# Which engine issues the two turned copies of the second softmax's weights: ScalarE instead of SyncE

## The chip, the cores and the metric

One Trainium2 chip, one of its cores. The metric is device time in microseconds (us), the median over runs of the whole program. The kernel is a single launch; all its intermediate arrays stay on the chip or in its own HBM buffers.

## The reference

Three computations follow one another. The inputs have 8 batches, 8 heads, 576 rows and head dimension 64; 32 "packed" queries stand in `p`.

```python
def sm_attn(qq, kk, vv):
    s = scale * np.matmul(qq, kk.transpose(0, 1, 3, 2))
    s = s - np.max(s, axis=-1, keepdims=True)
    a = np.exp(s)
    a = a / (np.sum(a, axis=-1, keepdims=True) + 1e-09)
    return np.matmul(a, vv)
p_packed = sm_attn(p, k, v)              # first softmax: 32 packed rows per head
out = sm_attn(q, p_packed, p_packed)     # second softmax: 576 rows over 32 columns
# x = out as [4608, 512]
rms = np.sqrt(np.mean(x * x, axis=-1, keepdims=True) + 1e-06)
xn = x / rms * rms_g
g = xn @ w_gate; val = xn @ w_val        # d_ff = 1536
y = (g / (1 + np.exp(-g)) * val) @ w_out
final = ((y @ w1) * (y @ w2) @ w3) @ w_out2
```

The attention's output is never built: the kernel multiplies the packed values into the gate and value weights (tiles `wbh`, `wbl`) and multiplies these by the second softmax's transposed, normalised weights `a2T` (split into `ah`, `al`). The RMS of a row is found from the softmax weights as well, with a small Gram matrix `G` of the packed values: the sum of squares of a row is a2T * (G a2T), summed over 32 columns and 8 heads.

## The kernel before, in words

The order of the work on every engine is written out by hand (`manual_schedule`, line 76): each engine runs its instructions strictly in the order in which the Python program issues them, and that holds for DMA issues too. Every DMA of the kernel is issued by SyncE (SP). A DMA that has to wait for data therefore holds back every DMA that comes after it in the program.

The stretch that matters is the first third, some 20 to 460 us, in which attention and the gate/value layer run together for batch after batch:

- `dense_units` (lines 418 to 454) is the main loop. One batch has 48 steps, here called units and numbered on through the batches. A unit is six matmuls of 128x288 (line 432) into one of four PSUM banks (`bank`, line 55). An even unit ends in a tanh on ScalarE (ACT, line 438) and a multiply on VectorE (DVE, line 439, "stt" below); an odd one, from batch 1 on, in a copy on ACT (line 447, tile `vl`) and a multiply on GpSimd (POOL, line 448, tile `ht`), in batch 0 in a multiply on DVE (line 444). After the fourth unit of each group of eight, `wb_unit` (lines 383 to 397) makes the next group's weights: matmuls on line 391, then `split` (lines 58 to 60), that is `wbh` on ACT (line 59) and `wbl` on DVE (line 60). Results `ht` go to HBM by `store_later` and `stores` (lines 402 to 409).
- `unpack(b)` (lines 284 to 378) is the second softmax of batch b. It is a generator with 18 steps, and `planned` (lines 490 to 497) takes its steps between the units of the batch before, at the numbers in `PLAN` and `UNPACK` (lines 533 to 542). Steps 0 to 6 compute the scaled exponentials. Step 7 transposes one half of them on DVE (line 327, e = 1) and issues the two copies that the change is about (lines 330 and 331). Step 8 transposes the other half (e = 0). Step 9 multiplies by `G` on TensorE (PE, line 343), sixteen matmuls by `a2T` and sixteen by `turned`, and takes the products on DVE (line 348).
- `turned` is `a2T[:, 1]` moved up by 32 partitions, the last 32 rows last, so that the matmuls of both halves can sit in different quarters of the array. It is made for batches 1 to 7, so there are 14 copies: seven of 96 rows and seven of 32, each row 2304 bytes. `turned` has one buffer.
- `pack(b)` (lines 202 to 279) is the first softmax; its last step copies `G` on ACT (line 277), its first has reductions on DVE (line 218) and exponentials on ACT (line 221).
- Weights come as 64-bit words and are converted: load (line 106), two ACT instructions (lines 113 and 114), two on DVE (lines 120 and 121), one on POOL (line 123).

In the program's order step 7 of `unpack` stands right behind the tanh of one unit: unit 20 for batch 1, unit 76 for batch 2, and units 112, 160, 208, 256 and 304 for batches 3 to 7. Step 8 follows at once for batches 3 to 7, at unit 21 for batch 1 and at unit 79 for batch 2. Step 9 stands behind unit 24 for batch 1, unit 81 for batch 2, and units 119, 167, 215, 263 and 311 after that. For batch 2, step 0 of `pack(3)` stands at unit 78, between steps 7 and 8.

After about 460 us the output projection and the bilinear layers follow; nothing in them is touched.

Of the kernel before, what the change touches and what calls it, by code (L numbers as in the profile page):

```python
# [32 lines left out]
def packed_attention_swiglu_bilinear(ctx: ExitStack, tc, qT, kT, v, v_end, pT, rms_g, w_gv, w_out,  # L33
                                     w1, w2, w3T, w_out2, out):
    nc = tc.nc
# [248 lines left out]
    def unpack(b):  # L284
# [21 lines left out]
        for a, t in enumerate(ts):  # L306
            nc.vector.transpose(out=a2.rearrange("p e t n -> p e (t n)")[:, :, HALF * a:HALF * a + HALF],
                                in_=t[:, :, :HALF])
# [15 lines left out]
        a2T = att.tile([128, 2, S], F32, tag="a2T", name="a2T")  # L324
        order = (0, 1) if b == 0 else (1, 0)
        for e in order:
            nc.vector.transpose(out=a2T[:, e], in_=a2[:, e].rearrange("p t n -> p (t n)"))
            if b and e:
                turned = att.tile([128, S], F32, tag="turned", name="turned")
                nc.sync.dma_start(out=turned[:96], in_=a2T[32:, 1])  # L330
                nc.sync.dma_start(out=turned[96:], in_=a2T[:32, 1])
            yield

        assert ("made", b) in over
# [184 lines left out]
    def spin():  # L519
        while True:  # L520
            t = bank()
            for _ in range(4):
                nc.tensor.matmul(t[:, :128], lhsT=ident, rhs=ident, start=True, stop=True)
            yield

    gens = dict(x=spin(), p=pack(0), u=unpack(0), c=gvw, d=gvd, w=wb_first(), l=later(), P=pack(1), U=unpack(1),
                Q=pack(2), V=unpack(2), R=pack(3), o=ow)
    for x in ("pxxpxdxcxppdpcdpccdxcuduudcxuldupuxcuuw"
              "xxxxxdxlcuxxxxxxdcuuduuuPxlPPluPuxuuPldP"):
# [16 lines left out]
    for b in range(2, B - 1):  # L546
        if b + 2 < B:
            steps.append(([48 * b + n for n in PACK], pack(b + 2)))
        steps.append(([48 * b + n for n in UNPACK], unpack(b + 1)))
        steps.append(([48 * b + n for n in WOUT], ow))  # L550
# [560 lines left out]
```

## Time and profile before

| what | value |
|---|---|
| median of 3 runs | 1348.25 us (1348.1 to 1349.21) |
| the profiled execution: its own time | 1346.48 us |
| its span, first to last instruction | 1344.6 us |
| mean granted TensorE clock | 0.996 |
| busy: PE / DVE / ACT / POOL | 98% / 65% / 43% / 41% |
| PE's tenths in the 40 slices | 7 in the first, 8 in the third and the last, 9 or more else |
| granted clock's tenths in the 40 slices | 8 in the third slice (67 to 101 us), 9 or more else |

The page gives busy time by engine, the span in 40 slices, the DMA queues, the chain of waits that ended last, and the costliest groups of instructions. Of the trace, timelines of single engines, the waits of one tile, the chain of waits in a window and busy time by stretch are used below. In a timeline the bracket behind a row is the engine's idle time before it and what ended it. SPq is SyncE's queue of DMA issues.

### The profile page before, as it was taken

The numbers are of one execution on the slowest core, as the hardware profiler recorded it, in microseconds if no ns is written. First come the engines' busy times: TensorE is split into PE (matmuls) and PEld (weight loads), VectorE is DVE, ScalarE is ACT, GpSimd is POOL, SyncE is SP. The second block draws the span as 40 slices with busy tenths as digits, with TensorE's granted clock in tenths as the row PEclk, the third lists the DMA queues.
The fourth block names the chain that finished last, engine by engine and source line by source line (L and its number), as shares of the span: only waits on it lengthen the run. The fifth ranks groups of instructions, "written<-read, shape, count | busy, mean of one in ns | idle before, by whom it ended". The sixth has DMA issues, their size and how long they took to land.

```text
span 1344.6 us, 23644 instructions
## 1 busy us (share of the span) xinstructions
PE 1322.6 (98%) x9010; PEld 1124.2 (84%) x9010; DVE 875.4 (65%) x1286; ACT 577.7 (43%) x1117; POOL 557.4 (41%) x467
## 2 busy tenths in 40 slices
PE   7989999999999999999999999999999999999998
PEld 6768888888888888888888888888888888899998
DVE  5796677777776557727475664578459657657645
ACT  5645566667666655525243442124015103305113
POOL 3341446656556542203221313445345335435442
PEclk9989999999999999999999999999999999999999
DMA  9855467647342576724399885656755856787875
GB/s 342 305 187 199 152 219 255 218 160 265 125 160 104 166 243 225 241 81 156 107 379 388 316 278 210 223 209 225 263 203 200 287 187 219 249 299 262 282 272 185
DMA packets 88706, 304.04 MB, mean 226 GB/s; under 512 B 9872, under 2 KB 14992, under 8 KB 74384
## 3 DMA queue, kind: packets, MB, share of 16 engines
q1 hardware_dynamic: 88592, 302.52, 63.9%
q8 instruction: 71, 1.16, 0.4%
q14 instruction: 43, 0.35, 0.1%
HBM read 223.87 MB, written 76.55 MB: 223 GB/s over the span
## 4 chain that ended last, share of the span: by engine, by line
PE 88%; DVE 7%; DMA 2%; issue 2%; ACT 1%; POOL 0%; SPq 0%; DVEq 0%; ACTq 0%; POOLq 0%
PE gv L432 21%; PE gv L946 13%; PE at L946 13%; PE at L636 12%; PE gv L636 7%; PE gv L1040 5%; PE at L1040 5%; PE at L391 3%; PE gv L736 3%; DVE sl L60 1%; PE at L214 1%; DVE wbl L60 1%; PE at L343 1%; PE at L245 1%; PE at L359 1%
## 5 line engine op out<-in xcount | busy, mean ns | idle before, releaser
L448 POOL TENSOR_TENSOR ht<-th,vl 128x288 f32<-128x288 f32 x168 | 138.9, 836 | 121.2 <-ACT vl L447 68.9
L432 PE MATMUL gv<-ah,wbh 128*128 128x288 f32 x768 | 174.5, 308 | 4.6 <-DVE th L439 3.9
L432 PEld LDWEIGHTS gv<-ah,wbh 128*128 128x128 f32 x768 | 121.2, 188 | 55.9 <-issue 22.5
L432 PE MATMUL gv<-al,wbh 128*128 128x288 f32 x768 | 164.7, 295 | 0.0
L432 PE MATMUL gv<-ah,wbl 128*128 128x288 f32 x768 | 164.1, 295 | 0.0
L60 DVE TENSOR_TENSOR hl<-hr,hh 128x512 fp32r<-128x512 f32 x108 | 101.3, 943 | 75.1 <-ACT hh L59 72.9
L972 POOL TENSOR_TENSOR s<-uc 128x512 f32<-128x512 f32 (+1 forms) x40 | 49.0, 1224 | 231.6 <-DVE uc L928 231.6
L946 PE MATMUL gv<-xh,w 128*128 128x512 f32 (+1 forms) x560 | 137.8, 367 | 0.0
L946 PE MATMUL at<-xh,w 128*128 128x512 f32 (+1 forms) x560 | 137.7, 367 | 0.0
L123 POOL TENSOR_TENSOR c_o<-c_o,c_y 128x512 int32<-128x512 int32 x52 | 71.0, 1366 | 146.2 <-DVE c_o L121 124.8
L439 DVE SCALAR_TENSOR_TENSOR th<-th,gv 128x288 f32<-128x288 f32 x192 | 84.9, 445 | 61.6 <-ACT th L438 52.4
L432 PEld LDWEIGHTS gv<-al,wbh 128*128 128x128 f32 x768 | 123.4, 188 | 0.0
L432 PEld LDWEIGHTS gv<-ah,wbl 128*128 128x128 f32 x768 | 123.3, 188 | 0.0
L59 ACT ACTIVATE hh<-hr 128x512 fp32r<-128x512 f32 x108 | 67.6, 629 | 115.2 <-PE at L636 60.1
L946 PEld LDWEIGHTS gv<-xh,w 128*128 128x128 f32 x560 | 102.5, 188 | 13.4
L946 PEld LDWEIGHTS at<-xh,w 128*128 128x128 f32 x560 | 102.5, 188 | 13.3
L636 PE MATMUL at<-hl,wo_h 128*128 128x512 f32 x288 | 112.1, 389 | 0.0
L636 PE MATMUL at<-hh,wo_l 128*128 128x512 f32 x288 | 112.1, 389 | 0.0
L636 PE MATMUL at<-hh,wo_h 128*128 128x512 f32 x288 | 112.0, 389 | 0.0
L438 ACT ACTIVATE th<-gv 128x288 f32<-128x288 f32 x192 | 78.7, 410 | 53.2 <-PE gv L432 51.8
L447 ACT ACTIVATE vl<-gv 128x288 f32<-128x288 f32 x168 | 69.2, 412 | 50.1 <-PE gv L432 35.1
L60 POOL TENSOR_TENSOR xl<-yi,xh 128x1024 fp32r<-128x1024 f32 (+1 forms) x20 | 57.3, 2872 | 74.0 <-ACT xh L59 49.9
(164 smaller groups left out, 2836.1 us busy)
## 6 DMA issues: line engine op xcount, KB each, us to landing
w<-ws_d SPq DMA_DIRECT2D x40, 1024.0 KB, 5.0
w<-w_d SPq DMA_DIRECT2D x35, 1024.0 KB, 4.8
w<-ws_d SPq DMA_DIRECT2D x40, 768.0 KB, 4.6
hT_d<-ht SPq DMA_DIRECT2D x96, 288.0 KB, 3.5
hr<-hT_d SPq DMA_DIRECT2D x108, 256.0 KB, 4.9
w<-in_w_gv_dram SPq DMA_DIRECT2D x24, 512.0 KB, 6.1
w<-in_w_out_dram SPq DMA_DIRECT2D x20, 512.0 KB, 5.0
q<-in_qT_dram SPq DMA_DIRECT2D x8, 1152.0 KB, 7.6
```

What stands on the lines that cost most here:

```text
L59: nc.scalar.activation(out=hi, in_=src, func=AF.Copy)
L60: eng_lo.tensor_tensor(out=lo, in0=src, in1=hi.bitcast(F32), op=ALU.subtract)
L123: nc.gpsimd.tensor_tensor(out=d, in0=d, in1=shape(y), op=ALU.add)
L432: nc.tensor.matmul(t[:, :HALF], lhsT=w[:, e, 256 * i + 128 * f:256 * i + 128 * f + 128], rhs=x[:, e, HALF * hf:HALF * hf + HALF], start=(n ...
L438: nc.scalar.activation(out=th, in_=t[:, :HALF], func=AF.Tanh, scale=0.5)
L439: nc.vector.scalar_tensor_tensor(out=th, in0=th, scalar=1.0, in1=t[:, :HALF], op0=ALU.add, op1=ALU.mult)
L447: nc.scalar.activation(out=vl, in_=t[:, :HALF], func=AF.Copy, scale=0.5)
L448: nc.gpsimd.tensor_tensor(out=ht[:, hf], in0=th, in1=vl, op=ALU.mult)
L636: nc.tensor.matmul(acc[m], lhsT=w[:, kk, 128 * m:128 * m + 128], rhs=x, start=(kk == 0 and a == 0), stop=(kk == NF - 1 and a == 2))
L946: nc.tensor.matmul(t, lhsT=wi[:, r, pos, a], rhs=x[:, j, r, :w], start=(start and at == 0), stop=(at == 5), skip_group_check=True)
L972: nc.gpsimd.tensor_tensor(out=s2, in0=u2, in1=c22, op=ALU.mult)
L1040: nc.tensor.matmul(t, lhsT=wi[:, s, k, 128 * m:128 * m + 128], rhs=x, start=(j in (0, 5, 4, 3) and k == 0 and n == 0), stop=(k == 3 and n ...
```

## The change

The two copies into `turned` are issued by ScalarE's queue. Source, destination and place in the program stay as they are; the copies now stand in ACT's order, behind the tanh of the unit named above and ahead of the next ACT instruction, and no longer in SyncE's.

```diff
             nc.vector.transpose(out=a2T[:, e], in_=a2[:, e].rearrange("p t n -> p (t n)"))
             if b and e:
                 turned = att.tile([128, S], F32, tag="turned", name="turned")
-                nc.sync.dma_start(out=turned[:96], in_=a2T[32:, 1])
-                nc.sync.dma_start(out=turned[96:], in_=a2T[:32, 1])
+                nc.scalar.dma_start(out=turned[:96], in_=a2T[32:, 1])
+                nc.scalar.dma_start(out=turned[96:], in_=a2T[:32, 1])
             yield
```

## Rows read from the trace of the kernel before

**Rows 1.** The page, busy us (share of the span) and instructions by engine.
```profile
PE 1322.6 (98%) x9010; PEld 1124.2 (84%) x9010; DVE 875.4 (65%) x1286; ACT 577.7 (43%) x1117; POOL 557.4 (41%) x467
```
**Rows 2.** The page, the chain that ended last, shares of the span by engine.
```profile
PE 88%; DVE 7%; DMA 2%; issue 2%; ACT 1%; POOL 0%; SPq 0%; DVEq 0%; ACTq 0%; POOLq 0%
```
**Rows 3.** Tile `turned`: count, ns min/median/max, first and last start; landing in us.
```profile
L330 SPq DMA_DIRECT2D turned<-a2T x7: 527/532/583, 81.7 to 409.1; - x7
L331 SPq DMA_DIRECT2D turned<-a2T x7: 587/587/594, 82.3 to 409.7; - x7
...
DMA to landing us min/median/max: 2.5/2.7/3.0
```
**Rows 4.** Waits of SyncE's queue, 60 to 440 us: total, times, longest.
```profile
SPq L330 <- DVE a2T L327: 40.8, 5, 8.2
```
**Rows 5.** Timeline of DVE, batch 2's copies: start, length, instruction, idle before.
```profile
148.05 0.77 DVE L327 STREAM_TRANSPOSE a2T<-a 128x576 f32<-128x576 f32 x1
148.74 0.42 DVE L439 SCALAR_TENSOR_TENSOR th<-th,gv 128x288 f32<-128x288 f32 x1
...
150.87 0.77 DVE L327 STREAM_TRANSPOSE a2T<-a 128x576 f32<-128x576 f32 x1
152.58 0.46 DVE L439 SCALAR_TENSOR_TENSOR th<-th,gv 128x288 f32<-128x288 f32 x1 [0.94 <-ACT th L438]
```
**Rows 6.** Timeline of ACT around batch 2's copies.
```profile
147.97 0.41 ACT L438 ACTIVATE th<-gv 128x288 f32<-128x288 f32 x1 [0.32 <-PE gv L432]
...
151.78 0.40 ACT L447 ACTIVATE vl<-gv 128x288 f32<-128x288 f32 x1
152.07 0.41 ACT L438 ACTIVATE th<-gv 128x288 f32<-128x288 f32 x1
```
**Rows 7.** Chain of waits, 140 to 160 us: start, length, what.
```profile
151.78 1.38 PE at L343 x31
```
**Rows 8.** Timeline of SyncE's queue around batch 3's copies.
```profile
195.07 0.59 SPq L331 DMA_DIRECT2D turned<-a2T  x1
```
**Rows 9.** Timeline of ACT around batch 3's copies.
```profile
194.40 0.41 ACT L438 ACTIVATE th<-gv 128x288 f32<-128x288 f32 x1 [0.33 <-PE gv L432]
...
196.28 1.03 ACT L59 ACTIVATE wbh<-at 128x1024 fp32r<-128x1024 f32 x1
197.20 0.41 ACT L438 ACTIVATE th<-gv 128x288 f32<-128x288 f32 x1
```
**Rows 10.** Timeline of DVE around batch 3's copies.
```profile
197.34 1.23 DVE L60 TENSOR_TENSOR wbl<-at,wbh 128x1024 fp32r<-128x1024 f32 x1 [0.78 <-ACT wbh L59]
198.49 0.44 DVE L439 SCALAR_TENSOR_TENSOR th<-th,gv 128x288 f32<-128x288 f32 x1
```
**Rows 11.** Timeline of PE after batch 3's copies.
```profile
199.49 0.45 PE L343 MATMUL at<-turned,G 32*32 32x288 f32 x4
...
200.60 0.53 PE L432 MATMUL gv<-ah,wbh 128*128 128x288 f32 x2
```
**Rows 12.** Timeline of ACT around batch 1's copies.
```profile
76.86 0.42 ACT L438 ACTIVATE th<-gv 128x288 f32<-128x288 f32 x1
...
78.55 0.25 ACT L277 ACTIVATE G<-at 128x64 f32<-128x64 f32 x1
82.87 0.41 ACT L438 ACTIVATE th<-gv 128x288 f32<-128x288 f32 x1 [4.07 <-PE gv L432]
```
**Rows 13.** Chain of waits, 60 to 110 us.
```profile
83.89 2.24 PE at L343 x24
...
90.80 6.02 DMA hT_d<-ht
```
**Rows 14.** Timeline of DVE around the landing of that store.
```profile
96.95 0.46 DVE L444 SCALAR_TENSOR_TENSOR ht<-th,gv 128x288 f32<-128x288 f32 x1 [1.89 <-DMA hT_d<-ht]
```
**Rows 15.** Stretches: PE, PEld, DVE, ACT, POOL busy; granted clock, DMA share, GB/s.
```profile
78.00:82.00 4.00, 2.03 (x10) 1.80 (x11) 3.90 (x8) 0.80 (x3) 2.32 (x2) 0.88 0.00 0
81.00:83.90 2.90, 1.81 (x8) 1.50 (x9) 2.87 (x6) 0.97 (x2) 1.12 (x1) 0.51 0.29 90
```

## The prediction, made before the run

> **What bounds the kernel now.** I read the page's busy times first: PE is busy 98% of the span, every other engine 65% or less [rows 1]. The chain that ended last agrees, 88% of it is PE, and SyncE's queue has 0% [rows 2]. So a moved DMA issue saves nothing by itself, and what the change is worth is decided where PE waits. Next I took the waits of the tile `turned`. An issue takes SyncE 0.53 and 0.59 us, and the copies land 2.5 to 3.0 us after it [rows 3]. Then the waits of SyncE's queue: at five of the seven places it stands at line 330 for up to 8.2 us until DVE has made the transpose [rows 4]. SyncE has nothing else to do; ACT has. Last I read the timelines of ACT, DVE and PE at the seven places, because after the change ACT must stand still from the tanh ahead of the copies until the transpose is there, and for the two issues besides.
>
> **What is removed.** Seven times two issues leave SyncE, 7 x 1.12 = 7.8 us of its time, and its five long waits, 40.8 us [rows 3, 4]. All of it lies off the chain. What stood behind them (stores of `ht`, loads of weight words) can be issued sooner.
>
> **What is added to ACT, per place.** The wait for the transpose, then the two issues. In the trace the second issue starts 0.6 us after the first (82.3 after 81.7) and takes 0.59, so SyncE's pair takes 1.2 us [rows 3]. No ACT issue is in the trace. Bounds: 0, if ACT handed the issues on and went ahead at once, and 2.4, twice SyncE's pair, if an engine with work of its own in flight issues more slowly. I take 1.2, the same instruction's own row.
>
> **Batch 2, the term that decides.** Step 7 stands behind the tanh of unit 76, and the `vl` copy of unit 77, the tanh of unit 78 and everything after them now wait. The transpose ends at 148.05 + 0.77 = 148.82 [rows 5]; with 1.2 ACT is free at 150.02. The `vl` copy goes first, and the tanh follows 0.29 later, the spacing of the same two instructions at 151.78 and 152.07 [rows 6]: the tanh of unit 78 starts at 150.31 and not at 147.97. DVE's multiply (stt) starts 0.51 after a tanh that it waits for (152.07 to 152.58) [rows 5, 6], so at 150.82 and not at 148.74: 2.08 later. Behind it in DVE's order are the reductions of `pack(3)` and the second transpose at 150.87, with no idle time before it [rows 5], so the second transpose ends 2.08 later, and it is the one that PE's line 343 waits for at 151.78, where the chain of waits goes from DVE to PE [rows 7]. PE has no bracket of idle time there now, it will have one of 2.1 us, and after it PE is busy without slack. **+2.1**; with a pair of 0 it is +0.9, with 2.4 it is +3.3. The turned copies are not late then: their issues end at about 150.0 in both kernels, and 3.0 us after the second one's start they have landed [rows 3], ahead of 153.9.
>
> **Batches 3 to 7: five places with the same order, covered barely.** Batch 3's rows stand for all. SyncE's second issue ends at 195.07 + 0.59 = 195.66 [rows 8], and ACT's would too. Then it has one `vl` copy (0.29), and from the tanh at 194.40 to `wbh` at 196.28 there are 1.88 us without a gap [rows 9], so `wbh` starts at 195.66 + 2.17 = 197.83, 1.55 late, and so do the next tanh and DVE's `wbl`. `wbl` would start at 198.89 and the stt behind it at 198.49 + 1.55 = 200.04, ending at 200.48 [rows 10]. PE's next group starts at 200.60 [rows 11]; it needs `wbl` and the bank that this stt empties. Slack 0.1 us: **0 each**, and whatever the pair costs above 1.3 us comes out of PE five times over. The copies end their issue when they ended before and land about 197.6; they are first read at 199.49 [rows 3, 8, 11], 1.9 us of cover. I put **+0.2** for the five, since a slack of 0.1 is within what I can read.
>
> **Batch 1.** ACT runs far ahead of DVE here. The tanh of unit 20 starts at 76.86 and the copy of `G` ends at 78.80; ACT then idles 4.07 us [rows 12]. After the change ACT stands from 77.3 until the issues end at 82.3 + 0.59 = 82.9 [rows 3], and then still has this work, 1.94 us less the tanh's own 0.3: 1.6. `G` is ready at 84.5, line 343 starts 0.7 later than 83.89 [rows 13]. But 7 us on, the chain of waits leaves the engines: a store of `hT_d` issued at 90.80 takes 6.02 us to land [rows 13] and holds DVE's next `ht`, idle for 1.89 us [rows 14]. The DMA engines had stood at 0.00 from 78 to 82 [rows 15], while SyncE's queue waited at line 330. Loads that stood behind it start earlier now, so the store meets a shorter queue. Late by 0.7, some 0.9 with what DVE adds, and early by 0 to 1.9, DVE's idle time there: between -1.0 and +0.9. **0.**
>
> **Sum.** 2.1 + 0.2 + 0 = 2.3 us on the profiled execution's 1346.48: 1348.8. The median of the runs shown lies 1.77 above that execution, so I predict 1348.25 + 2.3 = **1350.5 us**, slower by 0.17%. What a measurement of this kernel can tell from no change is about 0.2%, 2.7 us; the forecast is a loss just inside it.
>
> A rule for the transfers: SyncE's copies land 2.5 to 3.0 us after issue [rows 3]. The Trainium skill ("DMA: Bandwidth & Descriptors", section "Issuing engines are not separate DMA queues") says that DMAs issued from different engines run on the same 16 DMA engines and interleave, so that issuing from several only saves the issue time. By that rule alone the copies land as before and the sum would be 0, rival C below. The rule counts what the issuing engine no longer does; SyncE's 8.2 us of standing [rows 4] show that an engine also pays with its wait, and by those rows the sum is 2.3.
>
> **Rivals.**
> - *A, every place stops PE.* If the pair on ACT takes 2.0, two thirds of the way to its upper bound, batch 2 costs 2.9, and each of batches 3 to 7 0.8 - 0.1 = 0.7: 2.9 + 3.5 + 0.3 for batch 1 = 6.7, so 1354.9. For it: the slack of 0.1 that I found at five places. Against: it needs ACT slower at an issue than SyncE. It decides from a pair of 1.3 us on.
> - *B, the clock falls.* PE's new 2.1 us of idle time at batch 2 are followed by small matmuls. At batch 1 the granted clock stood at 0.51, the 1.2 GHz level, from 81.0 on, after a stretch in which PE was busy 2.03 of 4.00 us [rows 15]. Then line 343's 1.38 us [rows 7] and about as much behind it take double: 2.3 + 1.4 to 2.8, about 1352.6. Against: PE is fully busy ahead of batch 2.
> - *C, ACT's standing is hidden and the time stays.* If issues on ACT let the next instruction through, batch 2 costs 0.9, which batch 1's earlier loads can pay: 1348.3. For it: ACT is busy 43% only [rows 1]. Against: DVE's row without a gap behind the tanh at batch 2.
> - *D, faster.* SyncE's queue, no longer held, brings the store of 90.80 in 1.9 us earlier and takes as much from each of some further stores that POOL waits for; with batch 2 at 0.9 that is at least 2.8 us off: 1345.4. It decides where the store lands before about 95. Against: PE is the chain nearly throughout [rows 2], so there is little left for POOL to give.
>
> **Chances.** Forecast 0.50 (its own range 1349.0 to 1351.8: a pair between 0.3 and 1.4, and batch 1's spread), A 0.18, B 0.10, C 0.16, D 0.06. The forecast's upper third lies past 2.7 us: slower 0.16 + 0.18 + 0.10 = 0.44. Within 0.2%: 0.34 + 0.16 = 0.50. Faster: 0.06. The range that leaves out D and the far part of A is 1347.6 to 1354.5.
>
> **What would show it.** ACT rows at line 330 and 331 with a wait up to the transpose and a pair of about 1.2 us; at batch 2 a PE gap of about 2 us before line 343 (151 to 154 us) with the second transpose some 2.1 us later; no PE gap before line 432 after line 343 at batches 3 to 7; SyncE's queue without a wait at line 330 and the store of about 91 us landing in under 6 us. I am wrong if the gap at batch 2 is under 1 us, if gaps of over 0.3 stand at batches 3 to 7, or if the granted clock falls anywhere past 100 us.

## The result, and the profile after

| what | before | changed |
|---|---|---|
| median, us | 1348.17 (1347.98 to 1349.21) | 1360.54 (1359.15 to 1361.12, 4 runs) |
| ratio, 95% interval | | 1.0093 [1.0081, 1.0105] |
| span of the profiled execution, us | 1344.6 | 1358.8 |

The change costs 12.4 us. The prediction said 2.3, with a range up to 1354.5: right in sign, wrong by a factor of five.

The page after: busy times, the granted clock in 40 slices, the new DMA queue (packets, MB, share), the chain by engine.

```profile
PE 1333.2 (98%) x9010; PEld 1130.3 (83%) x9010; DVE 873.7 (64%) x1286; ACT 575.3 (42%) x1117; POOL 558.9 (41%) x467
...
PEclk9889899999999999999999999999999999999999
...
q10 hardware_dynamic: 1120, 2.07, 0.5%
...
PE 84%; DVE 5%; DMA 2%; issue 1%; ACT 1%; ACTq 0%; SPq 0%; DVEq 0%
```

Beside [rows 1, 2] this looks like the same kernel: ACT is no busier and its queue has 0% of the chain. PE is "busy" 10.6 us longer with as many instructions: most of the loss hides there, as matmuls that take longer, and not as idle time.

To find the places, I cut both executions at the end of each batch's first transpose into `a2T` (start plus length in DVE's timelines, as 148.05 + 0.77 in [rows 5]):

| stretch, us | before | changed | more |
|---|---|---|---|
| start to batch 1's transpose (no copy yet) | 81.66 | 83.77 | +2.1 |
| batch 1 to 2 | 67.16 | 67.61 | +0.5 |
| batch 2 to 3 | 45.64 | 53.38 | +7.7 |
| batches 3 to 7, four stretches | 54.32, 54.31, 54.32, 51.60 | 55.13, 55.26, 54.96, 52.26 | +0.8, +0.9, +0.6, +0.7 |
| batch 7's to the end | 935.6 | 936.4 | +0.8 |

The first line isn't the change's: it ends before the first copy, and over all kernels profiled here, SyncE's or ACT's copies, that point lies between 81.4 and 84.4. (Near 42 us the granted clock is at half for 3.41 us in the profile before, for 6.83 in the changed one, and not at all in two of the others.) The rest is 0.5 for batch 1, 7.7 for batch 2 and 3.9 for batches 3 to 7: 12.1.

**Batch 2.** ACT's timeline of the changed kernel, to be read against [rows 6]:

```profile
148.98 0.40 ACT L438 ACTIVATE th<-gv 128x288 f32<-128x288 f32 x1
151.42 0.55 ACTq L330 DMA_DIRECT2D turned<-a2T  x1
152.01 0.61 ACTq L331 DMA_DIRECT2D turned<-a2T  x1
152.73 0.41 ACT L447 ACTIVATE vl<-gv 128x288 f32<-128x288 f32 x1 [3.35 <-PE gv L432]
153.03 0.41 ACT L438 ACTIVATE th<-gv 128x288 f32<-128x288 f32 x1
```

DVE's, against [rows 5]:

```profile
150.61 0.77 DVE L327 STREAM_TRANSPOSE a2T<-a 128x576 f32<-128x576 f32 x1
153.47 0.45 DVE L439 SCALAR_TENSOR_TENSOR th<-th,gv 128x288 f32<-128x288 f32 x1 [2.08 <-ACT th L438]
...
155.55 0.77 DVE L327 STREAM_TRANSPOSE a2T<-a 128x576 f32<-128x576 f32 x1
```

ACT stands from 149.38 until the transpose is there (150.61 + 0.77) and then for its pair, 151.42 to 152.62. The tanh, DVE's multiply and the second transpose come late one after the other. That much is the predicted chain. PE's timeline shows what it led to. First the row ahead of line 343 in the profile before, which ends 0.15 us ahead of that line's start at 151.78 [rows 7]; then the changed kernel:

```profile
151.21 0.42 PE L432 MATMUL gv<-ah,wbl 128*128 128x288 f32 x2
```

```profile
156.47 0.45 PE L343 MATMUL at<-a2T,G 32*32 32x288 f32 x4 [2.22 <-DVE a2T L327]
...
158.29 0.68 PE L343 MATMUL at<-turned,G 32*32 32x288 f32 x1 [1.00 <-DMA turned<-a2T]
158.30 0.71 PE L343 MATMUL at<-a2T,G 32*32 32x288 f32 x4
...
160.35 0.85 PE L432 MATMUL gv<-ah,wbh 128*128 128x288 f32 x2
```

Three losses stand in these rows: the gap of 2.22 that was predicted; a second gap of 1.00 for a copy that isn't there; and, from 157.76 on, matmuls of 0.85 that take 0.53 elsewhere [rows 11]. The last is the clock, in the stretch's granted value (columns as in [rows 15]):

```profile
157.76:168.00 10.24, 8.91 (x56) 5.67 (x56) 3.24 (x7) 3.23 (x6) 2.23 (x3) 0.50 0.15 55
```

For 10.24 us TensorE runs at 0.50, its 1.2 GHz level. For the second gap SyncE's queue and the landings point to a cause; the run that holds SyncE, below, tests it. SyncE's k load before, then the changed kernel's timeline:

```profile
151.23 0.40 SPq L87 DMA_DIRECT2D k<-in_kT_dram  x1
```

```profile
151.76 0.33 SPq L87 DMA_DIRECT2D k<-in_kT_dram  x1
152.18 0.57 SPq L106 DMA_DIRECT2D w<-in_w_out_dram  x1
```

The DMAs issued from 151 to 159 us: KB each, and us from issue to landing:

```profile
k<-in_kT_dram SPq DMA_DIRECT2D x1, 1152.0 KB, 6.3
...
w<-in_w_out_dram SPq DMA_DIRECT2D x1, 512.0 KB, 7.0
turned<-a2T ACTq DMA_DIRECT2D x1, 216.0 KB, 3.3
turned<-a2T ACTq DMA_DIRECT2D x1, 72.0 KB, 6.2
```

SyncE, no longer held by the copies, issues its k load 0.25 us ahead of ACT's second copy; before, the load went out 2.4 us behind the transpose's end and behind both copies. ACT's second copy, the smallest of the four transfers, takes 6.2 us to land and not 2.5.

**Batches 3 to 7.** Line 343's first and last rows at batch 3 before ([rows 11] have a row between):

```profile
199.47 0.45 PE L343 MATMUL at<-a2T,G 32*32 32x288 f32 x4
...
200.25 0.42 PE L343 MATMUL at<-turned,G 32*32 32x288 f32 x4
```

The changed kernel, ACT's first issue and PE's timeline:

```profile
204.79 0.53 ACTq L330 DMA_DIRECT2D turned<-a2T  x1
```

```profile
209.78 0.69 PE L343 MATMUL at<-a2T,G 32*32 32x288 f32 x8
210.64 0.44 PE L343 MATMUL at<-turned,G 32*32 32x288 f32 x4 [0.17 <-DVE wbl L60]
210.67 0.44 PE L343 MATMUL at<-a2T,G 32*32 32x288 f32 x4
...
211.15 0.66 PE L343 MATMUL at<-turned,G 32*32 32x288 f32 x8
```

DVE's row that releases it:

```profile
209.36 1.23 DVE L60 TENSOR_TENSOR wbl<-at,wbh 128x1024 fp32r<-128x1024 f32 x1 [0.62 <-ACT wbh L59]
```

Line 343 starts 4.99 us after the first issue (204.79), as before. But before, the matmuls of `turned` start 0.02 behind those of `a2T` and run beside them; here they start 0.86 later, at `wbl`'s end (210.59). The products of `a2T` go to one slot of `at` and those of `turned` to the other; the second slot still holds the projected weights that `wbl` reads. From its first start to its last end line 343 takes 2.03 us here and 1.84 to 2.15 at the five places, against 1.20 before. Hardly a bracket shows it, since PE is busy with the first half. The waits of the tile `turned` do, on the weight loads' side; before the change this view has no such line:

```profile
  DVE wbl L60: 3.7, 7
```

3.7 us in seven waits, all of them at these five places, which lose 3.9 in all.

### The profile page after: what moved, and what is told of

It is laid out like the page before. It is cut to its first block, busy times and chain, and to the rows that moved or that the text cites. A ratio compares the mean times of both kernels' runs of the same rounds, so it can differ in the third digit from the quotient of the medians.

```text
span 1358.8 us, 23626 instructions
## 1 busy us (share of the span) xinstructions
PE 1333.2 (98%) x9010; PEld 1130.3 (83%) x9010; DVE 873.7 (64%) x1286; ACT 575.3 (42%) x1117; POOL 558.9 (41%) x467
## 3 DMA queue, kind: packets, MB, share of 16 engines
q10 hardware_dynamic: 1120, 2.07, 0.5%
## 4 chain that ended last, share of the span: by engine, by line
PE 84%; DVE 5%; DMA 2%; issue 1%; ACT 1%; ACTq 0%; SPq 0%; DVEq 0%
PE gv L432 19%; PE gv L946 13%; PE at L946 13%; PE at L636 12%; PE gv L636 7%; PE at L1040 5%; PE gv L1040 5%; PE gv L736 3%; PE at L391 3%; DVE sl L60 1%; PE at L343 1%; DVE wbl L60 1%; DMA hr<-hT_d 1%; PE at L245 1%; DVE hl L60 1%
```

## The experiments

Theory T, from here on: three mechanisms, each at its own place. At batch 2, ACT's standing makes a first gap, the freed SyncE a second, and the clock falls behind them; at batches 3 to 7 it is the slot; at batch 1 nothing lasts.

**The change in parts.** In place of the two `nc.sync` lines stands the following, with the condition `b == 2`, `b > 2` or `b == 1`:

```diff
-                nc.sync.dma_start(out=turned[:96], in_=a2T[32:, 1])
-                nc.sync.dma_start(out=turned[96:], in_=a2T[:32, 1])
+                eng = nc.scalar if b == 2 else nc.sync
+                eng.dma_start(out=turned[:96], in_=a2T[32:, 1])
+                eng.dma_start(out=turned[96:], in_=a2T[:32, 1])
```

> Copies of batch 2 alone on ACT. Theory T (the loss is made at the places, batch 2 the largest): PE waits 2.2 us for DVE's second transpose and 1.0 for the 32-row copy ahead of line 343, and the granted clock stands at 0.5 for some 10 us behind it, which is 7.7 of the 14.2 us of the profiles: +6 to +8.5 us. Rival Q (a second hardware queue in use costs about 2 us wherever it is used, and the rest is spread evenly over the seven places, 1.7 each): +3.5 to +4.

> Copies of batches 3 to 7 alone on ACT. T: at each of the five places line 343 stands 0.65 to 0.95 us in the middle, for the PSUM slot that wbl on DVE has not read yet: +3.3 to +4.7 us, no fall of the clock. Q: +2 and five times 1.7: about +10.

> Copies of batch 1 alone on ACT. T: line 343 starts 0.8 later, the later store wait takes most of it back, 0 to +1 us; up to +2.5 if the clock at 0.5 near 85 us lasts longer, as it did with all copies moved. Q: +3.5 to +4.

A fourth run moves none of the copies, only one small load at the start, so that the second queue exists:

```diff
-    nc.sync.dma_start(out=gT, in_=rms_g)
+    nc.scalar.dma_start(out=gT, in_=rms_g)
```

> All copies on SyncE as before; only the load of the four columns of rms_g at the start is issued by ACT, so that a second hardware queue is in use and nothing waits for it. T: 0, within 1 us. Q: +2 us, the amount by which the profile of the changed kernel was late before its first copy.

| ACT issues | median, us | ratio to before (1346.55) |
|---|---|---|
| batch 2's copies | 1353.86 | 1.0054 [1.0036, 1.0072] |
| batches 3 to 7's | 1351.56 | 1.0032 [1.0021, 1.0043] |
| batch 1's | 1349.13 | 1.0009 [0.9999, 1.0020] |
| one other load | 1347.84 | 1.0002 [0.9993, 1.0012] |

(The ratio is estimated from all runs; it is not the quotient of the two medians.) By the ratios the first three add up to 7.3 + 4.3 + 1.2 = 12.8 us; the whole change has 12.4. So no sign shows that the parts help or hurt each other, and the second queue by itself costs nothing that can be told. Rival Q's 3.5 to 4, 10, 3.5 to 4 and 2 us stand outside all four intervals. PE's gaps with batch 2 alone:

```profile
153.16 0.70 PE L344 MATMUL at<-a2T,G 32*32 32x288 f32 x4 [2.22 <-DVE a2T L327]
...
155.01 0.68 PE L344 MATMUL at<-turned,G 32*32 32x288 f32 x1 [0.53 <-DMA turned<-a2T]
```

The stretch at the lower clock there, columns as above:

```profile
152.95:159.78 6.83, 6.09 (x43) 3.40 (x43) 1.63 (x4) 1.62 (x6) 1.58 (x2) 0.50 0.46 167
```

The stretch from batch 2 to 3 is 6.0 longer; the gaps, less the 0.15 that before has there, are 2.6 of it. Of the other 3.4 the clock has about 3.0, half of the 6.09 us in which PE was busy at 0.50; that is an estimate, and 0.4 stays open.

**The gap filled.** Batch 2's copies on ACT, and 16 products of the identity, into a bank that is not read, ahead of line 343:

```diff
+        if b == 2:
+            t = bank()
+            for _ in range(16):
+                nc.tensor.matmul(t[:, :128], lhsT=ident, rhs=ident, start=True, stop=True)
```

> Batch 2's copies on ACT as in the run with batch 2 alone (1353.9 us, +7.3), and 16 small matmuls of the identity on PE in the 2.2 us in which it waits ahead of line 343; their result is not used. Theory T (of batch 2's loss some 3 us are standing, the rest is the granted clock that falls to 0.5 behind the standing): the clock stays at 1 past 150 us, and +2.5 to +4 is left. Rival S (the clock falls because of the small 32x32 matmuls and whatever late data does, not because PE stood still): no change, +6 to +8.

1351.85 us, 1.0029 [1.0018, 1.0040]. PE:

```profile
154.13 3.73 PE L340 MATMUL gv<-ident 128*128 128x128 f32 x32
...
158.83 0.42 PE L348 MATMUL at<-turned,G 32*32 32x288 f32 x1 [0.33 <-DMA turned<-a2T]
```

The filler is 1.5 us longer than the gap, and yet the stretch is 1.8 shorter than without it (49.90 against 51.67): the granted clock is 1.00 from 101 to 1350 us. The clock's part is real: 1.8 + 1.5 = 3.3 us by the two traces, 4.9 by the times (7.3 less 3.9, and the 1.5).

**The wait without the issues.** SyncE's copies stay; behind them ACT reads one column of the same transpose, so that it stands as long but issues nothing:

```diff
+                seen = att.tile([128, 1], F32, tag="seen", name="seen")
+                nc.scalar.activation(out=seen, in_=a2T[:, 1, :1], func=AF.Copy)
```

> All copies on SyncE as before; at the same place ACT gets one tiny activation that reads a column of the transposed half, so ACT waits for the transpose and issues nothing. T (ACT's standing delays what is behind it): at batch 2 line 343 waits 2.2 less the 1.2 to 1.5 of the issues, 0.7 to 1.0; at batches 3 to 7 wbl is 0.3 to 0.6 late and the 0.9 us of slack of its PSUM slot hold; the clock stays: +0.5 to +2. Rival W (the waits alone are the loss, the issues are free): +10 to +12.

1346.93 us, 1.0001 [0.9992, 1.0011], before 1347.74. PE's row at batch 2:

```profile
151.78 0.45 PE L345 MATMUL at<-a2T,G 32*32 32x288 f32 x4 [1.05 <-DVE a2T L327]
```

The gap is 1.05 and not 0.15: +0.9, the figure that the prediction had for a pair of 0. No place of batches 3 to 7 loses anything (54.31 to 54.32 again). The wait alone costs at most 1.5 us, so rival W falls; what breaks the slack at batches 3 to 7 comes with the issues.

**The issues without the wait.** All copies on ACT, each behind work that ACT does after the transpose anyway: one step later in the lists of due units (22 at batch 1, 78 at batch 2, 20 at batches 3 to 7, where line 343's step goes from 23 to 26):

```diff
-                nc.sync.dma_start(out=turned[:96], in_=a2T[32:, 1])
-                nc.sync.dma_start(out=turned[96:], in_=a2T[:32, 1])
             yield
+            if b and (e == 0 if b != 2 else e == 1):
+                nc.scalar.dma_start(out=turned[:96], in_=a2T[32:, 1])
+                nc.scalar.dma_start(out=turned[96:], in_=a2T[:32, 1])
+                yield
...
-            ("U", [13, 15, 15, 16, 17, 18, 19, 20, 21, 24, 25, 28, 32, 34, 42, 42, 43, 45]),
+            ("U", [13, 15, 15, 16, 17, 18, 19, 20, 21, 22, 24, 25, 28, 32, 34, 42, 42, 43, 45]),
...
-            ("V", [63, 64, 67, 68, 72, 72, 73, 76, 79, 81, 82, 82, 84, 84, 87, 89, 91, 94]),
+            ("V", [63, 64, 67, 68, 72, 72, 73, 76, 78, 79, 81, 82, 82, 84, 84, 87, 89, 91, 94]),
...
-    UNPACK = [-1, -1, 0, 2, 7, 8, 12, 16, 16, 23, 24, 25, 30, 30, 35, 36, 38, 43]
+    UNPACK = [-1, -1, 0, 2, 7, 8, 12, 16, 16, 20, 26, 26, 26, 30, 30, 35, 36, 38, 43]
```

> All 14 copies on ACT, but at places where ACT need not wait for the transpose: batch 1 two units later (behind the copy of G), batch 2 two units later (behind the tanh of unit 78), batches 3 to 7 four units later (behind wbh), and there step 9 three units later, at 26. T (the place in ACT's order is the loss, not the queue): 0 to +1 us. Rival Q (copies on ACT's queue cost by themselves, ACT's time of 1.3 us per pair and late landings among SyncE's loads): +4 or more.

1357.67 us, 1.0077 [1.0063, 1.0090]: T's number missed by far. PE's waits from 100 to 460 us (total, times, longest) say why:

```profile
PE at L245 <- DVE sq L350: 4.2, 4, 1.0
PE at L345 <- DMA turned<-a2T: 2.6, 1, 2.6
PE at L393 <- DVE sq L350: 1.2, 1, 1.2
```

The five waits for `sq` are my own: with line 343's step at 26, the next user of `at` (`pack`'s line 245, once line 393) finds its slot still to be read by `sq`. The wait for the DMA is news. At batch 2 ACT stands under 0.5 us for the transpose (147.20 to 147.67), line 343 starts on time, and in its middle PE stands 2.65 us for the copy of 32 rows, which again landed 6.1 us after its issue, with the clock at half from 156.12 for 6.83 us. So the late landing needs no long standing of ACT. Rival Q had named it, "late landings among SyncE's loads", and at this place it is right against T: SyncE's k load went out ahead of that copy here too, at 148.01 against 148.26.

Of this kernel batch 1 alone was run too, at unit 22, with SyncE's copies everywhere else:

> Batch 1's copies alone on ACT, two units later, behind the copy of G; the others on SyncE as before. ACT idles there for 4 us anyway, and SyncE's loads no longer stand behind the copies. T: line 343 as early as before, and the store that DVE waits for near 97 us lands sooner: 0 to -1.5 us. Rival Q (SyncE's queue was never what held DVE, the DMA engines were): 0, within 0.3.

1348.04 us, 1.0002 [0.9993, 1.0011]. Without ACT's standing batch 1 costs nothing that can be told, and no gain from the freed queue shows (rival D); the interval leaves room for 0.9 us of it.

**SyncE held as before.** Batch 2's copies on ACT, and a copy of 32 bytes on SyncE that waits for the same transpose:

```diff
+                if b == 2:
+                    dummy = att.tile([1, 8], F32, tag="dummy", name="dummy")
+                    nc.sync.dma_start(out=dummy, in_=a2T[:1, 1, :8])
```

> At batch 2 alone ScalarE issues the two copies, at the place of the change; SyncE issues in their place a copy of 32 bytes that reads the same transpose, so that its k load (1152 KB) starts about when it did before. T (the copy of 32 rows lands late because SyncE's load is issued ahead of it or beside it): it lands about 3.2 us after the first issue's start, not 6.8; PE has one gap, of 2.2 us ahead of line 343, and none in it for `turned`; if the clock then falls the loss is 2 + 3, else 2: +1 to +5. Rival L (the ACT queue is slow by itself at this place): it still lands after 6 us and the second gap of 0.5 to 1.0 stays.

1350.41 us, 1.0019 [1.0010, 1.0028], before 1348.02. SyncE's k load with batch 2 alone, then SyncE's queue in this run:

```profile
148.37 0.33 SPq L87 DMA_DIRECT2D k<-in_kT_dram  x1
```

```profile
151.16 0.76 SPq L335 DMA_DIRECT2D dummy<-a2T  x1
152.03 1.18 SPq L413 DMA_DIRECT2D hT_d<-ht  x2
153.30 0.48 SPq L87 DMA_DIRECT2D k<-in_kT_dram  x1
```

The landings of `turned` and PE at line 343:

```profile
DMA to landing us min/median/max: 2.5/2.6/3.0
```

```profile
156.27 0.69 PE L347 MATMUL at<-a2T,G 32*32 32x288 f32 x8 [2.22 <-DVE a2T L327]
156.56 0.45 PE L347 MATMUL at<-turned,G 32*32 32x288 f32 x4
```

The k load goes out 0.9 us behind the second copy's issue (151.8 + 0.60), every copy lands within 3.0, the second gap is gone, and the first stands as it was. The stretch is 2.28 longer and no more: no clock falls. Rival L, an ACT queue that is slow by itself, falls. The k load stands 2.17 us behind the transpose's end here, 0.37 with batch 2 alone: these 1.8 us are worth 4.9 of batch 2's 7.3 us by the medians, 3.8 of 6.0 by the two traces.

The same with the copies at unit 78:

> As the run above, but the two issues stand in ACT's order at unit 78, behind the second transpose's place, where ACT waits for nothing. T (batch 2's loss is the wait on ACT, the late landing and the clock that falls behind both): with all three gone the PE gap ahead of line 343 is 0.9 to 1.1 as before, no gap for `turned`, no clock below 1.0 past 100 us, time -1 to +1. Rival L (the queue is slow by itself): a gap of 2.6 at line 343 or in it and a clock that falls, +3 to +5.

1347.33 us, 0.9997 [0.9988, 1.0006]: all of batch 2's loss is gone, with both copies still issued by ACT (the stretch is 45.72 against 45.64, with no gap at line 343 in PE's rows; the gap "of 0.9 to 1.1 as before" in the expectation was a slip, before has 0.15).

**Half the issue.** At batches 3 to 7 ACT issues the copy of 32 rows only:

```diff
                 nc.sync.dma_start(out=turned[:96], in_=a2T[32:, 1])
-                nc.sync.dma_start(out=turned[96:], in_=a2T[:32, 1])
+                eng = nc.scalar if b > 2 else nc.sync
+                eng.dma_start(out=turned[96:], in_=a2T[:32, 1])
```

> At batches 3 to 7 ScalarE's queue issues only the copy of 32 rows; SyncE issues the other, and both at batches 1 and 2. T (ACT is held by the issues; wbl comes late by as much and still holds one of the two slots of `at` that line 343 needs, so the second half of line 343 no longer runs beside the first): ACT is held 0.6 us and not 1.2, of which the slack takes all or nearly all. Line 343, from its first start to its last end, lasts 1.2 to 1.5 us at each of the five places (1.20 before, 1.84 to 2.15 changed); the time is +0 to +1.5. Rival S, a price for each issue without slack: 1.5 to 1.7 us each, +1.6 to +2.4. Rival Q, a second queue costs the same however little it carries: 1.85 and more, +3 to +4.

1347.65 us, 1.0000 [0.9991, 1.0009]. Line 343 at batch 3:

```profile
201.81 0.45 PE L344 MATMUL at<-a2T,G 32*32 32x288 f32 x4
201.90 0.45 PE L344 MATMUL at<-turned,G 32*32 32x288 f32 x4
```

The second half starts 0.09 behind the first, against 0.86 with both copies; 1.20 to 1.29 us from first start to last end at all five places. Half the price, and no loss: the slack is between 0.6 and 1.2 us of ACT's time, and nearer 0.6. SyncE still stands for its own copy in this run, so the time alone does not part the halved issue from the held queue; PE's rows of the changed kernel do, where it is `wbl` that holds the second half, and so does the next run: there SyncE is free at three of the places and line 343 is not longer.

**Line 343 one unit later.** ACT issues at batches 3, 5 and 7, SyncE at the others; the step goes from 23 to 24:

```diff
-    UNPACK = [-1, -1, 0, 2, 7, 8, 12, 16, 16, 23, 24, 25, 30, 30, 35, 36, 38, 43]
+    UNPACK = [-1, -1, 0, 2, 7, 8, 12, 16, 16, 24, 24, 25, 30, 30, 35, 36, 38, 43]
```

> Line 343 of batches 3 to 7 is placed one unit later (24 for 23), and ScalarE issues both copies at batches 3, 5 and 7; SyncE issues them at 1, 2, 4 and 6, which are the comparison within the run. T (the slot of `at`): by then wbl has been read, so line 343 lasts 1.20 us at all five places, and batches 3, 5 and 7 take no more than 0.2 us longer than 4 and 6. Rival M (what is late is the tanh and the bank, wherever line 343 stands): 3, 5 and 7 lose 0.6 to 0.9 each in gaps elsewhere, and are 1.2 to 1.8 behind 4 and 6 in all.

1349.40 us, 1.0014 [1.0004, 1.0025], +0.5 to +3.4. PE at batch 3, with the weight load (PEld) that begins its last group:

```profile
198.36 0.43 PE L433 MATMUL gv<-ah,wbl 128*128 128x288 f32 x2
198.78 0.53 PE L433 MATMUL gv<-ah,wbh 128*128 128x288 f32 x2
198.78 0.30 PEld L433 LDWEIGHTS gv<-ah,wbh 128*128 128x128 f32 x2 [0.23 <-ACT vl L448]
...
199.90 0.45 PE L344 MATMUL at<-a2T,G 32*32 32x288 f32 x4
199.93 0.45 PE L344 MATMUL at<-turned,G 32*32 32x288 f32 x4
```

Line 343 takes 1.20 us at all five places: the slot no longer holds it. But T's bound of 0.2 fell, since the stretches behind batches 3 and 5 are 54.70 and 54.67 against batch 4's 54.31: 0.37 each is left, and behind batch 7 it is 0.8 to the end (936.39 against 935.60), 0.45 of it within the first 10 us. It lies in PE's group ahead of line 343, which starts 0.42 behind the last one, with line 343 another 1.12 behind (0.27 and 0.88 at batch 4). The trace names both waits there: the group's weight load waits 0.23 us for ACT's `vl`, which empties its bank (0.19 and 0.28 at batches 5 and 7), and its matmuls of `wbl` start at 199.44, 0.05 behind `wbl`'s end (198.16 + 1.23). So T was right on the slot and wrong that nothing else stood behind it; rival M was right on the bank, but its 0.6 to 0.9 each is twice what was measured at batches 3 and 5. No run took one of these waits away alone. No kernel here beats the one before.

## Why the prediction was wrong, step by step

- **What is removed, "off the chain", failed.** The prediction saw that what stood behind SyncE's waits could start sooner and took that for harmless or a gain. At batch 2 it is a k load of 1152 KB, which SyncE's wait had kept behind the copies. "The turned copies are not late then" rested on SyncE's own landings [rows 3], taken with SyncE's queue held. Price: 1.0 us of PE here, 2.65 where nothing else was late, and most of what the clock then took.
- **Rival B was put at 0.10 and 1.4 to 2.8 us; it happened and was larger.** "PE is fully busy ahead of batch 2" was the reason against it, and it was no protection. The half clock lasted 10.24 us, in which PE was busy 8.91: half of that is 4.5, and 7.7 less the two gaps (3.1 more than before) leaves 4.6. The prediction counted only line 343 and as much again; [rows 15] show the half clock from 81.0 to 83.9 but not its end, and it lasted 6.83 us there. Of the signs of being wrong that were set, this one came: a granted clock that falls past 100 us.
- **Batches 3 to 7, "slack 0.1", failed: 3.9 for 0.2.** The lateness was computed rightly and held against the wrong user. The working has `wbl` starting at 198.89, 4.43 behind the transpose's end (measured 4.60), so ending at 200.12. It compared that with PE's next group at 200.60; but `wbl` also frees a slot of `at`, and line 343 needs both at 199.49 [rows 11], 0.63 earlier. The measured loss is 0.6 to 0.9 each. Rival A's five losses are there, but not by its condition: the pair took 1.19 us at four of the places and 1.38 at one, not 2.0. The sign set for these places, a gap of PE over 0.3, missed them too: the brackets are 0.17 and 0.29 and none, because line 343 grew longer and PE did not stand.
- **The pair of 1.2 us was right** (151.42 to 152.62). So was **batch 2's first gap**: 2.22 less 0.15 is 2.07 for 2.1, by the predicted chain of tanh, multiply and transpose.
- **Batch 1 at 0 stands within its bounds, in part by luck.** Line 343 starts 0.8 later for `G` (0.7 predicted; its own terms give 84.5 less 83.89, 0.6); alone it measured -0.1 to +2.7 us, and 0.5 in the trace, in a stretch that lies between 66.1 and 68.6 in runs with SyncE's copies there. That a shorter queue gives it back was not shown: DVE still waits 1.62 us for that store, 1.89 before, and 0.67 in the run with one other load on ACT, where no copy moved. The run at unit 22 saw no gain.
- **The rule for the transfers.** The Trainium skill ("DMA: Bandwidth & Descriptors", "Issuing engines are not separate DMA queues") says that DMAs of all issuing engines run on the same 16 DMA engines and interleave. The copy of 72 KB that took 6.2 us beside SyncE's 1152 KB, and 3.0 at most with that load held back, agrees. Its sentence that several issuers "only save" issue time does not cover this case: what the relieved queue issues next took more than the relieved issue gave.

## What to carry to other kernels

Moving a DMA issue moves two streams: work behind it on the new engine comes later by the wait and the issue, and work behind it on the old engine comes sooner, onto the same DMA engines; ask of both what they meet. When something is late by x, list every user of what it frees, buffer slots first, and take the earliest. And price a new gap of 2 us on TensorE with the clock that may fall behind it: here that was more than the gap itself.

## What the runs showed that was not expected

- A wait that cost nothing was a guard: replaced by a 32-byte copy, SyncE's standing at line 330 was worth 4 to 5 us.
- After PE's gaps at batch 2 the granted clock was 0.50 for 10.24 us (changed kernel) and for 6.83 us (twice). Which gap brings a fall is not settled: with batch 2 alone it fell at 152.95, inside the first gap of 2.22; with SyncE held, a gap of 2.22 at the same place was followed by none, and 11 timed runs of that kernel stayed between 1348.95 and 1351.48, while the 5 without the hold lay between 1351.55 and 1356.34. The mean granted clock of the timed runs says the same: 0.991 to 0.994 in those 5, 0.995 or 0.996 in the 11 with the hold and in the 6 with the gap filled, 0.994 to 0.997 before.
- Line 343's two halves share TensorE: 1.20 us side by side, 1.84 to 2.15 one behind the other with brackets of 0.17 and 0.29 us at batches 3 and 4 and none at the other three. A loss of this kind is found in the length of a group, not in PE's idle time.
